# Scaling the norm's rows on ScalarE, and the norm's weights per partition behind the transposes

## The chip, the cores and the metric

The kernel runs on one core of a Trainium2 chip. A core has TensorE (PE: matrix products, written to PSUM), VectorE (DVE), ScalarE (ACT), GpSimd (POOL) and SyncE (SP, which here issues all the transfers). Each engine runs its own instructions strictly in the order in which they were issued and waits for the others by semaphores. The metric is the device time of one execution in microseconds; lower is better.

## What is computed

Three stages follow each other: a gated linear attention over 768 steps (2 batches, 8 heads of 40), a gated feed-forward layer behind an RMS norm, and a second feed-forward layer.

```python
y[:, :, t] = o * h_tilde / denom                        # attention, one step
x = attn_out.transpose(0, 2, 1, 3).reshape(1536, 320)   # tokens x (heads*40)
rms = np.sqrt(np.mean(x * x, axis=-1, keepdims=True) + 1e-06)
xn = x / rms * rms_g                                    # the norm, rms_g: 320 weights
g = xn @ w_gate                                         # 320 -> 1536
x = (g / (1 + np.exp(-g))) * (xn @ w_val) @ w_out       # 1536 -> 320
h = x @ w_in                                            # 320 -> 2048
out = np.maximum(0.01 * h, h) @ w_out2                  # 2048 -> 320
```

## The kernel before

The 1536 tokens are 12 tiles of 128 (`T` = 0 to 11, six chunks for each of the two batches). The attention is computed chunk by chunk; its result for a tile is `y`, with the tokens on the partitions and the 320 features along the row. The norm turns `y` into `xn`, PE transposes `xn` in three blocks of 128 columns into the PSUM tile `tp` (so that features lie on the partitions), and the result goes to `X`, split into a coarse part (`X[:, 0:3]`, the rounding to PE's fp32r format, done by ACT) and the rest (`X[:, 3:6]`, the difference, done by DVE). The third block holds the last 64 features twice: columns 320 to 383 of `xn` are a copy of columns 256 to 319.

The feed-forward layer takes the tiles in four groups of three (0-2, 3-5, 6-8, 9-11). An up-projection (line 646) is eight matmuls over the 384 tokens of a group, with three blocks of features in coarse and fine parts; the second matmul already reads the fine part of block 0, so a group can start only when all its three tiles have passed the norm.

All instructions are issued in one order written out by hand: `ORDER`, a list of some 1900 short tokens, played from the first to the last. A token is one helper with its indices, and the order on each engine is the order of its tokens. For one tile `T` the tokens of the norm are: `yr` (DVE: `y` divided by the denominator), `sq` (ACT: sum of squares), `y2.T.0` (DVE), `y2.T.1` (POOL: the power -0.5), `y2.T.2` (three small DVE instructions, which end in `z`, one scale per token), `xn` (line 488), `xc` (line 492), `tp` (line 499, PE), `xh` (line 503, ACT), `xl` (line 507, DVE). Between them stand the tokens of other tiles and stages; those the prediction comes to are:

- `p`, `av`, `inn`, `kv`: the attention's scores (DVE line 382), its products (PE lines 395, 405, 417); `eq` and `mask`: POOL's scaling of `eb` (line 359) and its masking of `Ab` (line 355); `st`, `cb`, `c`: the state C (DVE lines 426 and 428), its copy by ACT (lines 433 and 434), its decay on POOL (line 364); `arg`: ACT's exponentials (line 351);
- `U`, `T`, `E`, `M`, `S`, `L` with group and block of the hidden layer: up-projections (PE), tanh (ACT line 673), two products (DVE lines 678, 685), coarse and fine parts of the result (ACT line 694, DVE line 700); `D`: the down-projection (PE line 718);
- `a`, `r`, `b`: the unpacking of weights (ACT line 538 and DVE lines 536 and 540, then a coarse and a fine part); `id`: matmuls on a constant that nobody reads (line 226).

PSUM has buffers in pairs by tag. A `tp` tile takes a buffer of the tag "o" (for tiles 1 and 2 of the tag "gv"), which the attention's results of a tile (`o1`) use too, in turn. The norm's weights lie in `gb`, 128 x 320, the same row on every partition, fetched by one transfer (`dgb`, line 995).

Of the kernel before, what the change touches and what calls it, by code (L numbers as in the profile page):

```python
# [56 lines left out]
co.1.1.2 cv.1.1.2 cv.0.2.6 sq.0 y2.0.0 yr.1 wA.2 kv.1 dgb p.2.0 av.2.0 arg.2.1 y2.0.1 p.2.1 y2.0.2 k.2 sq.1 y2.1.0 a.2  # L57
y2.1.1 a.1 xn.0 a.2 arg.3.1 a.1 dq.3 qk.3 p.3.1 dq.4 cb.0 wB.1 a.2 xc.0 b.1 dsl y2.1.2 th.2 a.2 dr.2.6 da.4 mask.4.1
wA.4 xn.1 av.2.1 inn.2 y1.2 xc.1 id.1 st.1 abs.2 id.1 id.1 id.1 p.3.0 rec.2 tp.0 id.1 b.1 tp.1 dn.3 yr.2 dr.1.2
mask.4.0 dc.1.2 a.4 sq.2 b.1 y2.2.0 kv.2 xh.1 wR.3 th.3 de.3 dE.2.6 k.3 b.1 id.1 xh.0 xl.0 av.3.0 co.1.2.6 cv.1.2.6  # L60
xl.1 cb.1 y2.2.1 y2.2.2 r.3 qk.4 eq.3 av.3.1 inn.3 dv.1.2 xn.2 arg.4.0 xc.2 tp.2 abs.3 r.3 r.3 c.3 rec.3 dn.5 kv.3 a.4
xh.2 arg.4.1 xl.2 U.0.1.1 p.4.0 k.5 y1.3 da.5 a.4 st.3 U.0.1.0 cb.3 p.4.1 th.5 T.0.1 dn.4 th.4 mask.5.0 wA.3 yr.3 sq.3
a.4 E.0.1 mask.5.1 a.3 arg.5.1 dc.2.6 de.4 r.3 arg.5.0 y2.3.0 a.3 eq.4 M.0.1 av.4.0 av.4.1 inn.4 dq.5 qk.5 y2.3.1 y1.4
p.5.1 U.0.0.0 p.5.0 T.0.0 E.0.0 dv.2.6 U.0.0.1 M.0.0 da.6 mask.6.1 arg.6.1 de.5 wB.0 abs.4 dq.6 a.3 rec.4 mask.6.0
av.5.0 av.5.1 S.0.1 eq.5 y2.3.2 yr.4 S.0.0 inn.5 kv.5 abs.5 b.0 xn.3 rec.5 b.0 sq.4 y2.4.0 y2.4.1 arg.6.0 qk.6 L.0.1
p.6.1 U.0.2.0 p.6.0 U.0.2.1 T.0.2 E.0.2 c.2 y1.5 dq.7 b.0 c.5 st.5 qk.7 yr.5 y2.4.2 c.4 cb.5 sq.5 a.3 k.4 kv.4 id.1
xc.3 tp.3 xh.3 y2.5.0 y2.5.1 dq.8 xn.4 da.7 xc.4 M.0.2 wB.2 U.0.3.0 st.4 cb.4 y2.5.2 c.6 L.0.0 xn.5 xl.3 tp.4 xh.4
xl.4 U.0.3.1 S.0.2 xc.5 T.0.3 tp.5 xh.5 de.6 dn.6 av.6.0 E.0.3 xl.5 av.6.1 wB.3 M.0.3 L.0.2 eq.6 inn.6 abs.6 wA.5 b.0
b.3 U.1.0.0 T.1.0 E.1.0 U.1.0.1 M.1.0 U.1.1.0 da.8 U.1.2.0 b.3 mask.7.0 arg.7.0 p.7.0 dn.7 av.7.0 mask.7.1 arg.7.1
p.7.1 av.7.1 k.7 S.0.3 b.2 L.0.3 de.7 b.2 eq.7 S.1.0 b.2 inn.7 L.1.0 b.2 b.3 b.3 wB.4 rec.6 T.1.2 E.1.2 mask.8.1 a.5  # L70
da.9 mask.9.0 mask.9.1 b.4 qk.8 a.5 th.7 T.1.1 th.6 y1.6 D.0.0.2 E.1.1 D.0.0.1 K.0.0.1 U.1.2.1 M.1.2 U.1.1.1 arg.8.1
p.8.1 M.1.1 mask.8.0 D.0.0.0 S.1.1 L.1.1 yr.6 S.1.2 a.5 wA.7 U.1.3.0 a.5 L.1.2 arg.8.0 b.4 p.8.0 de.9 dq.9 kv.7 T.1.3
E.1.3 k.6 eq.9 kv.6 st.6 arg.9.1 cb.6 U.1.3.1 M.1.3 abs.7 a.7 dn.8 a.7 U.0.5.0 T.0.5 E.0.5 sq.6 qk.9 K.0.0.0 av.8.0
de.8 S.1.3 L.1.3 wB.7 k.8 av.8.1 a.7 a.7 wR.5 K.0.0.2 rec.7 b.4 b.4 eq.8 inn.8 wA.6 a.6 a.6 dn.9 c.7 wB.6 de.11 y2.6.0
y2.6.1 b.6 U.0.4.0 U.0.5.1 M.0.5 y1.7 yr.7 D.1.0.0 y2.6.2 arg.9.0 p.9.0 D.1.0.1 T.0.4 U.0.4.1 S.0.5 L.0.5 E.0.4
# [1020 lines left out]
```

## Time and profile before

| | |
|---|---|
| three timed executions | 445.22, 447.4 and 451.2 us; median 447.4 us |
| profiled execution | 449.2 us from the first to the last instruction, 9736 instructions |
| PE busy | 437.8 us (97%) |
| DVE busy | 365.8 us (81%) |
| ACT busy | 281.3 us (63%) |
| POOL busy | 102.1 us (23%) |

The profile shows one execution, and times in it run from its first instruction. What lies around that span is not shown for it; of the timed runs two are shorter than the span and one is longer. The norm's instructions lie between 31.7 us and 163.8 us; what follows is the two feed-forward layers. PE's busy share is high because its matmuls are pipelined and nearly always queued. The granted clock of PE is given as a share of 2.4 GHz.

### The profile page before, as it was taken

What the parts mean: (1) busy time and instruction counts of PE and PEld (TensorE: products, weight loads), DVE (VectorE), ACT (ScalarE), POOL (GpSimd) and SP (SyncE); (2) the same over time, 40 slices, a digit from 0 to 9 for tenths busy, and PEclk for the clock granted to TensorE, in tenths of its full rate; (3) what the DMA queues carried; (4) which work ended last, traced back from release to release, by engine and by line L of the source; (5) the groups of instructions that cost most, each with busy time, mean ns of one, the idle gap of its engine ahead of it and who ended that gap; (6) DMA issues with size and microseconds to landing.
All of it is one profiled execution on the core that took longest, in us unless ns stands there. A gap on an engine that the chain in (4) does not pass through costs nothing.

```text
span 449.2 us, 9736 instructions
## 1 busy us (share of the span) xinstructions
PE 437.8 (97%) x3720; PEld 415.7 (93%) x3720; DVE 365.8 (81%) x822; ACT 281.3 (63%) x709; POOL 102.1 (23%) x162
## 2 busy tenths in 40 slices
...
GB/s 267 316 265 283 251 287 119 265 232 82 248 88 77 56 0 175 78 83 0 124 1 1 1 1 0 1 1 153 30 31 76 107 47 32 31 29 31 0 2 176
DMA packets 21039, 45.47 MB, mean 101 GB/s; under 512 B 2128, under 2 KB 9168, under 8 KB 20992
## 3 DMA queue, kind: packets, MB, share of 16 engines
...
q8 instruction: 29, 0.48, 0.5%
q14 instruction: 18, 0.15, 0.1%
HBM read 42.79 MB, written 2.06 MB: 100 GB/s over the span
## 4 chain that ended last, share of the span: by engine, by line
PE 89%; DVE 6%; ACT 2%; issue 2%; DVEq 0%; ACTq 0%
PE h L796 13%; PE xa L718 10%; PE g L646 8%; PE v L646 8%; PE oa L969 6%; PE oa L968 6%; PE oa L967 6%; PE u L796 6%; PE xw L736 5%; PE s L335 3%; PE h L802 2%; PE h L801 2%; PE o L395 2%; PE busy L226 2%; PE o L405 1%
## 5 line engine op out<-in xcount | busy, mean ns | idle before, releaser
L969 PE MATMUL oa<-wB,xl 128*128 128x320 f32 x192 | 59.3, 309 | 0.0
L968 PE MATMUL oa<-wB,xh 128*128 128x320 f32 x192 | 59.3, 309 | 0.0
L967 PE MATMUL oa<-wB,xh 128*128 128x320 f32 x192 | 59.2, 308 | 0.0
L646 PE MATMUL g<-X,wA 128*128 128x384 f32 x256 | 50.7, 343 | 0.9 <-ACT th L671 0.4
L979 DVE TENSOR_TENSOR x<-oa,x 128x320 f32<-128x320 f32 x84 | 39.5, 484 | 14.6 <-PE oa L969 13.9
L646 PE MATMUL v<-X,wA 128*128 128x384 f32 x256 | 50.0, 339 | 0.1
L646 PEld LDWEIGHTS g<-X,wA 128*128 128x128 f32 x256 | 44.5, 189 | 2.9 <-ACT th L671 0.7
L718 PE MATMUL xa<-sh,wB 128*128 128x384 f32 x160 | 46.0, 338 | 0.0
L646 PEld LDWEIGHTS v<-X,wA 128*128 128x128 f32 x256 | 44.6, 188 | 0.7 <-DVE X L507 0.4
L578 POOL TENSOR_TENSOR sums<-w_A 128x128 f32<-128x128 f32 x8 | 3.9, 488 | 151.8 <-DVE w_A L540 146.6
L969 PEld LDWEIGHTS oa<-wB,xl 128*128 128x128 f32 x192 | 36.0, 188 | 0.1
L967 PEld LDWEIGHTS oa<-wB,xh 128*128 128x128 f32 x192 | 36.0, 188 | 0.0
L968 PEld LDWEIGHTS oa<-wB,xh 128*128 128x128 f32 x192 | 36.0, 188 | 0.0
L796 PE MATMUL h<-X,wA 128*128 128x384 f32 x144 | 32.2, 337 | 0.0
L718 PE MATMUL xa<-sl,wB 128*128 128x384 f32 x96 | 32.2, 336 | 0.0
L943 ACT ACTIVATE c<-c 128x384 f32<-128x384 f32 x48 | 25.2, 525 | 7.2 <-DVE c L840 3.4
L718 PEld LDWEIGHTS xa<-sh,wB 128*128 128x128 f32 x160 | 29.4, 188 | 0.1
L953 DVE TENSOR_TENSOR xl<-c,xh 128x384 fp32r<-128x384 f32 x48 | 26.1, 556 | 1.0 <-ACT xh L948 0.8
L948 ACT CAST xh<-c 128x384 fp32r<-128x384 f32 x48 | 24.3, 513 | 2.9 <-PE oa L968 2.2
L351 ACT ACTIVATE w<-Ab,aeu 128x128 f32<-128x128 f32 x80 | 25.3, 392 | 0.6 <-POOL Ab L355 0.6
L796 PEld LDWEIGHTS h<-X,wA 128*128 128x128 f32 x144 | 25.0, 188 | 0.1
L479 POOL TENSOR_TENSOR sm<-sm,mhalf 128x1 f32<-128x1 f32 x12 | 8.0, 663 | 65.0 <-DVE sm L477 65.0
...
## 6 DMA issues: line engine op xcount, KB each, us to landing
...
```

Source lines behind the costliest of these rows:

```text
L351: A.activation(w[:, j], src, AF.Exp, scale=-1.0, bias=col)
L646: PE.matmul(dst, a, x, start=(i == 0), stop=(i == len(seq) - 1))
L718: PE.matmul(xa, w, x, start=(k == 0), stop=(k == len(seq) - 1))
L736: PE.matmul(xas["w", g, i], a, x, start=(f == NE and k == 0), stop=(f == NF - 1 and k == len(seq) - 1),)
L796: PE.matmul(dst, x, y, start=first and j == 0, stop=j == 2, skip_group_check=not first)
L943: A.activation(t, src, AF.Prelu, alpha=0.01)
L948: A.copy(v["h"], v["t"])
L953: V.tensor_tensor(v["l"], v["t"], v["h"].bitcast(F32), op=ALU.subtract)
L967: PE.matmul(oa, v["h"][:, ts], wb[:, 0:DM], start=m == 0, stop=False)
L968: PE.matmul(oa, v["h"][:, ts], wb[:, DM:], start=False, stop=False)
L969: PE.matmul(oa, v["l"][:, ts], wb[:, 0:DM], start=False, stop=m == 1)
L979: V.tensor_tensor(dst, oas[k, p, i], dst, op=ALU.add)
```

## The change

Instead of DVE, ACT multiplies the rows of `y` by `z`, in two instructions (320 columns and the 64 that stand twice), each with one scale per partition. The weights come behind the transposes, where a feature is a partition: `gcol`, 128 x 3, one column per block. ACT's `xh` takes them as a scale in three instructions of 128 columns in place of one of 384, and DVE's `xl` multiplies by them and subtracts, also in three. The token `xc` is gone and `dgb` is `dgc`; the order of all other tokens is the same, and the two ACT instructions of the new `xn` stand where the old `xn` stood in the list.

```diff
-    gb = attc.tile([128, DM], F32, name="gb")
+    gcol = attc.tile([128, 3], F32, name="gcol")
...
     def att_xna(T):
...
-        V.scalar_tensor_tensor(out=xn[:, 0:DM], in0=t["yf"], scalar=t["z"], in1=gb, op0=ALU.mult, op1=ALU.mult)
-
-    def att_xnc(T):
-        xn = st_[T]["xn"]
-        A.copy(xn[:, DM:384], xn[:, 256:DM])
+        A.activation(xn[:, 0:DM], t["yf"], AF.Copy, scale=t["z"])
+        A.activation(xn[:, DM:], t["yf"][:, 256:], AF.Copy, scale=t["z"])
...
     def att_xh(T):
-        A.copy(X[:, 0:3, T * L:(T + 1) * L], st_[T]["tv"])
+        for k in range(3):
+            A.activation(X[:, k, T * L:(T + 1) * L], st_[T]["tv"][:, k], AF.Copy, scale=gcol[:, k:k + 1])
...
     def att_xl(T):
         tv, cs = st_[T]["tv"], slice(T * L, (T + 1) * L)
-        V.tensor_tensor(X[:, 3:6, cs], tv, X[:, 0:3, cs].bitcast(F32), op=ALU.subtract)
+        for k in range(3):
+            V.scalar_tensor_tensor(
+                out=X[:, 3 + k, cs], in0=tv[:, k], scalar=gcol[:, k:k + 1], in1=X[:, k, cs].bitcast(F32), op0=ALU.mult, op1=ALU.subtract,
+            )
...
-        dsl=lambda: Q.dma_start(out=sel, in_=cst2), dgb=lambda: Q.dma_start(out=gb, in_=rg.partition_broadcast(128)),
+        dsl=lambda: Q.dma_start(out=sel, in_=cst2), dgc=lambda: Q.dma_start(out=gcol, in_=rg),
...
-        "rg": c(moe_rms_g.reshape(DM)),
+        "rg": c(moe_rms_g[np.concatenate([s, s + 128, s % 64 + 256]).reshape(3, 128).T]),
```

In `ORDER` each of the twelve `xc` tokens is deleted, as here for tile 5:

```diff
-xl.4 U.0.3.1 S.0.2 xc.5 T.0.3 tp.5 xh.5
+xl.4 U.0.3.1 S.0.2 T.0.3 tp.5 xh.5
```

What stands in a row on ACT at tiles 3, 4 and 5, before (L470 is `sq.5`, L492 `xc`, L503 `xh`, L433 and L434 `cb.4`, L694 `S.0.2`, L673 `T.0.3`; xn_1043, xn_1144 and xn_1170 belong to tiles 3, 4 and 5):

```order
86 L470 ACTIVATE junk_1119,sm_1038<-y_1093 128x320
87 L492 COPY xn_1043<-xn_1043 128x64
88 L503 CAST X<-tp_1135 128x3x128
89 L492 COPY xn_1144<-xn_1144 128x64
90 L433 COPY Cbd_97<-C_95 64x4x41
91 L434 COPY Cbd_97<-C_95 40x4x41
92 L503 CAST X<-tp_1173 128x3x128
93 L694 CAST sh_2_1188<-th_2_1089 128x384
94 L492 COPY xn_1170<-xn_1170 128x64
95 L673 ACTIVATE th_3_1191<-g_3_1152 128x384
96 L503 CAST X<-tp_1193 128x3x128
```

And after (L488 and L489 are the new `xn`, L501 the new `xh`, L695 and L674 the old L694 and L673; xn_1158 belongs to tile 4 and xn_1184 to tile 5):

```order
91 L470 ACTIVATE junk_1132,sm_1050<-y_1106 128x320
92 L501 ACTIVATE X<-tp_1147,gcol 128x128 x3
93 L488 ACTIVATE xn_1158<-y_932,sm_974 128x320
94 L489 ACTIVATE xn_1158<-y_932,sm_974 128x64
95 L433 COPY Cbd_97<-C_95 64x4x41
96 L434 COPY Cbd_97<-C_95 40x4x41
97 L488 ACTIVATE xn_1184<-y_1106,sm_1050 128x320
98 L489 ACTIVATE xn_1184<-y_1106,sm_1050 128x64
99 L501 ACTIVATE X<-tp_1190,gcol 128x128 x3
100 L695 CAST sh_2_1209<-th_2_1102 128x384
101 L674 ACTIVATE th_3_1211<-g_3_1166 128x384
102 L501 ACTIVATE X<-tp_1213,gcol 128x128 x3
```

The copies of 64 columns are gone. The scaling of tile 4 stands between the `xh` of tile 3 and `cb.4`, that of tile 5 between `cb.4` and the `xh` of tile 4; tile 3's stands further up, behind line 539 of `b.0`.

What stands in a row on DVE at the same place, before (L481 to L483 are `y2.5.2`, L700 is `L.0.0`, L488 the old `xn` of tile 5, L507 the `xl` of tiles 3, 4 and 5, L678 `E.0.3`):

```order
142 L481 TENSOR_SCALAR sm_1038<-sm_1038 128x1
143 L482 TENSOR_SCALAR sm_1038<-sm_1038 128x1
144 L483 TENSOR_TENSOR sm_1038<-sm_1038 128x1
145 L700 TENSOR_TENSOR sl_0_1168<-th_0_933,sh_0_1012 128x384
146 L488 SCALAR_TENSOR_TENSOR xn_1170<-y_1093,sm_1038,gb 128x320
147 L507 TENSOR_TENSOR X<-tp_1135,X 128x3x128
148 L507 TENSOR_TENSOR X<-tp_1173,X 128x3x128
149 L678 SCALAR_TENSOR_TENSOR th_3_1191<-th_3_1191,g_3_1152 128x384
150 L507 TENSOR_TENSOR X<-tp_1193,X 128x3x128
```

And after (L506 is the new `xl`):

```order
137 L481 TENSOR_SCALAR sm_1050<-sm_1050 128x1
138 L482 TENSOR_SCALAR sm_1050<-sm_1050 128x1
139 L483 TENSOR_TENSOR sm_1050<-sm_1050 128x1
140 L701 TENSOR_TENSOR sl_0_1182<-th_0_945,sh_0_1024 128x384
141 L506 SCALAR_TENSOR_TENSOR X<-tp_1147,gcol,X 128x128 x3
142 L506 SCALAR_TENSOR_TENSOR X<-tp_1190,gcol,X 128x128 x3
143 L679 SCALAR_TENSOR_TENSOR th_3_1211<-th_3_1211,g_3_1166 128x384
144 L506 SCALAR_TENSOR_TENSOR X<-tp_1213,gcol,X 128x128 x3
```

Nothing stands between `L.0.0` and the `xl` of tile 3 any more.

## Rows read from the trace of the kernel before

**Rows 1.** Busy us (instructions) in three stretches: PE, PEld, DVE, ACT, POOL; clock, DMA, GB/s.

```profile
30.00:50.00 20.00, 17.89 (x289) 13.90 (x290) 16.77 (x49) 13.90 (x43) 8.99 (x16) 0.66 0.89 241
50.00:76.00 26.00, 23.51 (x445) 21.09 (x444) 25.19 (x56) 16.46 (x52) 14.24 (x20) 0.93 0.77 249
76.00:160.00 84.00, 84.00 (x1012) 80.86 (x1012) 63.93 (x162) 49.83 (x145) 16.79 (x27) 1.00 0.47 140
```

**Rows 2.** DVE's groups by line and shape: count, busy us, mean ns, idle before.

```profile
L488 DVE SCALAR_TENSOR_TENSOR xn<-y,sm,gb 128x320 f32<-128x320 f32 x12 | 9.2, 763 | 0.1
...
L507 DVE TENSOR_TENSOR X<-tp,X 128x384 fp32r<-128x384 f32 x12 | 6.5, 551 | 1.8 <-ACT X L503 1.8
...
L593 DVE TENSOR_TENSOR wA<-sums,wA 128x128 fp32r<-128x128 f32 x8 | 2.2, 281 | 0.0
```

**Rows 3.** ACT's groups by line and shape, 0 to 165 us.

```profile
L351 ACT ACTIVATE w<-Ab,aeu 128x128 f32<-128x128 f32 x80 | 25.3, 392 | 0.6 <-POOL Ab L355 0.6
...
L503 ACT CAST X<-tp 128x384 fp32r<-128x384 f32 x12 | 5.7, 477 | 4.0 <-PE tp L499 3.9
...
L439 ACT ACTIVATE nat<-nat 128x320 f32<-128x320 f32 x12 | 5.5, 465 | 0.1
...
L351 ACT ACTIVATE w<-A,aeu 128x128 f32<-128x128 f32 x16 | 4.5, 362 | 3.0 <-DVE x L231 1.6 <-PE pt L248 1.0 <-PE A L261 0.4
...
L492 ACT COPY xn<-xn 128x64 f32<-128x64 f32 x12 | 2.9, 241 | 6.2 <-DVE xn L488 6.2
```

**Rows 4.** The chain that ended last, 64 to 76 us: start, us, what.

```profile
67.42 2.63 issue
...
73.72 1.93 PE g L646 x8
```

**Rows 5.** All engines in order of time, 64 to 74 us, with idle time before.

```profile
65.13 0.48 ACT L503 CAST X<-tp 128x384 fp32r<-128x384 f32 x1 [0.53 <-PE tp L499]
...
66.04 0.33 ACT L433 COPY Cbd<-C 64x164 f32<-64x164 f32 x1 [0.28 <-DVE C L426]
...
66.59 1.65 PE L646 MATMUL v<-X,wA 128*128 128x384 f32 x8
...
66.95 3.17 DVE L488 SCALAR_TENSOR_TENSOR xn<-y,sm,gb 128x320 f32<-128x320 f32 x1
67.32 1.28 POOL L359 TENSOR_TENSOR eb<-eb,qkt 128x512 f32<-128x512 f32 x1
...
68.56 1.22 POOL L355 TENSOR_SCALAR_AFFINE_SELECT Ab<-Ab 128x512 f32<-128x512 f32 x2
...
70.73 0.64 PE L499 MATMUL tp<-consts,xn 128*128 128x128 f32 x3 [2.49 <-DVE X L507]
```

**Rows 6.** The same view, 40 to 52 us.

```profile
40.94 1.28 POOL L359 TENSOR_TENSOR eb<-eb,qkt 128x512 f32<-128x512 f32 x1 [0.46 <-DMA eb<-e_d]
...
41.25 0.56 DVE L507 TENSOR_TENSOR X<-tp,X 128x384 fp32r<-128x384 f32 x1 [0.70 <-ACT X L503]
...
49.70 1.29 POOL L359 TENSOR_TENSOR eb<-eb,qkt 128x512 f32<-128x512 f32 x1
49.76 1.58 DVE L464 TENSOR_TENSOR y<-y,sm 128x320 f32<-128x320 f32 x1
```

**Rows 7.** Windows again: PE's clock behind two pauses.

```profile
41.00:47.00 6.00, 6.00 (x126) 5.08 (x125) 3.79 (x13) 3.53 (x13) 1.85 (x2) 0.50 0.94 267
71.00:74.00 3.00, 3.00 (x100) 2.48 (x99) 2.59 (x6) 0.69 (x3) 1.19 (x3) 0.50 0.17 42
```

**Rows 8.** PE in order of time, 36 to 42 us.

```profile
37.13 0.55 PE L499 MATMUL tp<-consts,xn 128*128 128x128 f32 x3 [0.41 <-DVE C L428]
...
39.45 0.35 PE L295 MATMUL pg<-rG,sel 16*128 16x8 f32 x2 [1.22 <-issue]
```

**Rows 9.** The chain that ended last, 160 to 170 us.

```profile
162.83 0.38 ACT X L503
...
168.08 1.28 ACT L671
```

More of the change, by code (lines that the diff above doesn't have):

```diff
@@ L56 @@
 rec.0 wA.1 a.1 rec.1 r.2 dq.2 a.1 yr.0 id.1 mask.3.0 arg.3.0 r.2 id.1 r.2 qk.2 th.1 st.0 y1.1 de.2 dA.2.6 eq.2 ux.1.2
[L57 to L75, printed above, removed]
@@ new lines @@
+y2.1.1 a.1 xn.0 a.2 arg.3.1 a.1 dq.3 qk.3 p.3.1 dq.4 cb.0 wB.1 a.2 b.1 dsl y2.1.2 th.2 a.2 dr.2.6 da.4 mask.4.1 wA.4
+xn.1 av.2.1 inn.2 y1.2 id.1 st.1 abs.2 id.1 id.1 id.1 p.3.0 rec.2 tp.0 id.1 b.1 tp.1 dn.3 yr.2 dr.1.2 mask.4.0 dc.1.2
+a.4 sq.2 b.1 y2.2.0 kv.2 xh.1 wR.3 th.3 de.3 dE.2.6 k.3 b.1 id.1 xh.0 xl.0 av.3.0 co.1.2.6 cv.1.2.6 xl.1 cb.1 y2.2.1
+y2.2.2 r.3 qk.4 eq.3 av.3.1 inn.3 dv.1.2 xn.2 arg.4.0 tp.2 abs.3 r.3 r.3 c.3 rec.3 dn.5 kv.3 a.4 xh.2 arg.4.1 xl.2
+U.0.1.1 p.4.0 k.5 y1.3 da.5 a.4 st.3 U.0.1.0 cb.3 p.4.1 th.5 T.0.1 dn.4 th.4 mask.5.0 wA.3 yr.3 sq.3 a.4 E.0.1
@@ new lines @@
+mask.5.1 a.3 arg.5.1 dc.2.6 de.4 r.3 arg.5.0 y2.3.0 a.3 eq.4 M.0.1 av.4.0 av.4.1 inn.4 dq.5 qk.5 y2.3.1 y1.4 p.5.1
+U.0.0.0 p.5.0 T.0.0 E.0.0 dv.2.6 U.0.0.1 M.0.0 da.6 mask.6.1 arg.6.1 de.5 wB.0 abs.4 dq.6 a.3 rec.4 mask.6.0 av.5.0
+av.5.1 S.0.1 eq.5 y2.3.2 yr.4 S.0.0 inn.5 kv.5 abs.5 b.0 xn.3 rec.5 b.0 sq.4 y2.4.0 y2.4.1 arg.6.0 qk.6 L.0.1 p.6.1
+U.0.2.0 p.6.0 U.0.2.1 T.0.2 E.0.2 c.2 y1.5 dq.7 b.0 c.5 st.5 qk.7 yr.5 y2.4.2 c.4 cb.5 sq.5 a.3 k.4 kv.4 id.1 tp.3
+xh.3 y2.5.0 y2.5.1 dq.8 xn.4 da.7 M.0.2 wB.2 U.0.3.0 st.4 cb.4 y2.5.2 c.6 L.0.0 xn.5 xl.3 tp.4 xh.4 xl.4 U.0.3.1 S.0.2
@@ new lines @@
+T.0.3 tp.5 xh.5 de.6 dn.6 av.6.0 E.0.3 xl.5 av.6.1 wB.3 M.0.3 L.0.2 eq.6 inn.6 abs.6 wA.5 b.0 b.3 U.1.0.0 T.1.0 E.1.0
+U.1.0.1 M.1.0 U.1.1.0 da.8 U.1.2.0 b.3 mask.7.0 arg.7.0 p.7.0 dn.7 av.7.0 mask.7.1 arg.7.1 p.7.1 av.7.1 k.7 S.0.3 b.2
+L.0.3 de.7 b.2 eq.7 S.1.0 b.2 inn.7 L.1.0 b.2 b.3 b.3 wB.4 rec.6 T.1.2 E.1.2 mask.8.1 a.5 da.9 mask.9.0 mask.9.1 b.4
+qk.8 a.5 th.7 T.1.1 th.6 y1.6 D.0.0.2 E.1.1 D.0.0.1 K.0.0.1 U.1.2.1 M.1.2 U.1.1.1 arg.8.1 p.8.1 M.1.1 mask.8.0 D.0.0.0
+S.1.1 L.1.1 yr.6 S.1.2 a.5 wA.7 U.1.3.0 a.5 L.1.2 arg.8.0 b.4 p.8.0 de.9 dq.9 kv.7 T.1.3 E.1.3 k.6 eq.9 kv.6 st.6
```

186 lines of the change are left out of this document (95 added, 91 removed).

## The prediction

> **What bounds the kernel now.** I read the busy shares by stretch first, then the chain of work that ended last, then the timeline around each of the twelve tiles. The norm's instructions all lie before 164 us, and the stretches there differ [rows 1]. From 76 to 160 us PE is busy for 84.00 of 84 us at a granted clock of 1.00 (its 2.4 GHz level): nothing that DVE or ACT saves there is seen, as long as neither comes late. From 50 to 76 us DVE is busy for 25.19 of 26 us, ACT for 16.46, and PE misses 2.5 us. From 30 to 50 us PE misses 2.1 us and runs at 0.66 of the clock on average. So only 30 to 76 us, and the end of the stage at 160 to 170 us, can give or take time.
>
> Inside them one place stands out. From 67.42 us the chain goes through 2.63 us in which nothing that the profile shows was awaited [rows 4]. The timeline says what that is: DVE's `xn` of tile 5 stood there, from 66.95 us, and took 3.17 us [rows 5], where the twelve take 9.2 us together, so that the other eleven take (9.2 - 3.17) / 11 = 0.55 us each [rows 2]. While it stood, POOL ran `eq` and `mask` (67.32 to 69.78 us) without a gap. PE had finished its up-projection at 66.59 + 1.65 = 68.24 us and waited 2.49 us for the PSUM buffer of `tp.5`, which the `xl` of tile 3 gives back, and that `xl` stood behind this `xn` on DVE [rows 5]. After the pause PE was granted 0.50 (1.2 GHz) from 71 to 74 us, with work in all three of those us [rows 7]; at the other level this work takes half, so the pause cost another 1.5 us. This place alone is worth up to 2.49 + 1.5 = 4.0 us.
>
> Which DVE instructions POOL holds up is seen in two pairs [rows 6]. The `yr` at 49.76 us, beside POOL's line 359, took 1.58 us; it reads two tiles from SBUF. The `xl` at 41.25 us, inside the same POOL instruction of another tile, took 0.56 us, its usual time [rows 2]; it reads one tile from PSUM and one from SBUF. The old `xn` is of the first kind (`y` and `gb`).
> The Trainium skill (SBUF — State Buffer, Who interferes with whom) has a rule for this: a DVE instruction with two SBUF inputs contends with a GpSimd instruction that reads SBUF and waits for all of it, one with a single SBUF input does not. By it the stall leaves with the old `xn` and the sum below holds; without it the next DVE instruction could inherit the stall, and the first rival below would be the forecast. Both pairs agree with it.
>
> **The change part by part.**
>
> DVE, `xn` and `xl`. Removed: twelve `xn`, 0.55 us each, one of them 3.17 [rows 2, 5]. Added: each `xl` is three instructions of 128 columns in place of one of 0.551 us. No row shows this form; the nearest of that width took 0.281 us [rows 2], so three take between 0.55 us (no cost for the splitting) and 0.84 us. I take the upper end, +0.29 us. DVE gains about 0.26 us a tile, and the 2.6 us of the stall.
>
> ACT, `xn`. The 320 columns without a scale per partition took 0.465 us, 64 columns 0.241 us [rows 3]; on the line between them 128 columns would take 0.297 us, and line 351, which has one operand per partition (its bias), took 0.392 us. So such an operand costs 0.095 us here. New `xn`: 0.465 + 0.095 + 0.241 + 0.095 = 0.90 us, some 0.85 us with the overlap of neighbours; bounds 0.71 and 0.90. The old copy (0.24 us) goes.
>
> ACT, `xh`. Three of 128 columns out of PSUM: line 351 with PSUM input took 0.362 us alone and 4.5 / 16 = 0.28 us in a row [rows 3], so 0.36 + 2 x 0.28 = 0.92 us in place of 0.48; bounds 0.8 and 1.1. Together ACT gets some 1.0 to 1.3 us more per tile, 12 to 15 us in all, where it now has 16.46 us in 26 [rows 1]. ACT has room on average; the question is its order.
>
> The transfer. 160 KB of `gb` become 1.5 KB while the transfers are busy for 0.89 of their time [rows 1]. At 241 GB/s that is 0.7 us less traffic; no wait of PE in this stretch ends with a transfer, so I count nothing, between -0.7 and 0.
>
> **Place B, tiles 3 to 5 (60 to 76 us).** The old times are carried forward with the new durations. `xh.3` starts at 65.13 us, when PE has made `tp.3` [rows 5], and ends at 66.05. ACT then scales tile 4 until 66.9; `tp.4`, which before came just ahead of the up-projection at 66.59 us [rows 5], and that up-projection with it, come 0.5 us later. ACT copies the state (`cb.4`, two of 0.33 us [rows 5]), scales tile 5 until 68.4 us, and starts `xh.4`. DVE, without the old `xn`, starts `xl.3` at 67.0 us and is done at 67.8. PE's up-projection now ends at 68.24 + 0.5 = 68.75 us, and both things that `tp.5` needs, its rows (68.4) and its buffer (67.8), are there: the 2.49 us are gone. The next wait is that of `av.6` for the buffer of `tp.4`, which `xl.4` gives back: `xh.4` ends at 69.3 and `xl.4` at 69.6 us, `tp.5` at 69.1, so 0.5 us. Of POOL's work `inn.6` needs `eq.6`; that waits for `cb.4` and moves from 68.6 to 69.3 us, ahead of its use. Without a pause of two us the clock should hold. Sum: -2.49 - 1.5 + 0.5 + 0.5 = -3.0 us; the group's up-projection, at 73.72 us before [rows 4], starts some 2.7 us earlier and also runs at the higher clock. Bounds: -4.0 (no new waits) and 0 (the new waits are as long as the old one, and the clock falls with them).
>
> **Place A, tiles 0 to 2 (30 to 50 us).** PE waited 0.41 us at `tp.0` for DVE's copy of the state and 1.22 us ahead of line 295, which reads a product of DVE [rows 8]. Both DVE instructions stand behind the old `xn` of tiles 0 and 1, so they come up to 0.5 us earlier each time. But `arg.3.1` on ACT now stands behind the new `xn.0`, and `p.3.1` on DVE waits for it: the first saving is lost, the second stays. I take -0.4 us, the length of the first pause; bounds -1.6 (both pauses go) and +0.5 (`arg.4.0` stands behind `xn.2`, which waits for `z` of tile 2).
>
> **Place C, the end of the stage (160 to 170 us).** Here ACT is on the chain: `xh.11` at 162.83 us, then the unpacking of weights between ACT and DVE, up to the load of ACT's function table at 168.08 us [rows 9]. `xh.11` is 0.45 us longer and everything behind it moves: +0.5 us; bounds 0 (PE can start the group on the first block) and +0.8 (`xl.11` longer, too).
>
> From 76 to 160 us I count nothing: PE is never idle there [rows 1], and the slack of the six tiles' `xn` and `xh` is the time that ACT is free, 34 of 84 us, against some 8 us more work.
>
> Sum: -3.0 - 0.4 + 0.5 = -2.9 us on a span of 449.2 us. Median before 447.4 us, so **444.5 us**; bounds by the ends -5.6 and +1.3: 441.8 and 448.7 us. The profiled span lies 1.8 us above the median of the three timed executions, which themselves reach from 445.22 to 451.2; a difference of 2% (9 us) is about what this kernel's measurement tells from no change.
>
> **The rivals.**
>
> The next wait takes the gain. If the stall is not the two inputs' but POOL's hold on whatever DVE issues next, `xl.3` inherits it, or `tp.5` or `av.6` waits for something that the trace hides behind the old wait. For: DVE is busy for 25.19 of 26 us, so its relief of 0.26 us a tile buys little. Against: the undisturbed `xl` [rows 6]. Place B gives 0, A and C cancel: 447.4 us, 447 to 448.
>
> ACT becomes late, and the kernel slower. Place B again: `xn.5` now stands on ACT behind `xh.3`, `xn.4` and `cb.4`, and `tp.5` waits for ACT instead of DVE. It decides from the point at which ACT ends `xn.5` after 70.1 us, when the old one ended; I have 68.4, so ACT would have to be 1.7 us later than I think, for instance because it waits in order for a `z` that DVE or POOL brings late. Then the pause and the fall of the clock stay, the extra 0.5 us at `tp.4` and 0.5 us at C come on top, and another +0.5 us at `arg.4.0`, with at most 1.5 us for a second fall of the clock: +1.5 to +3, 449 to 450.5 us, taken as 449.7. Against it: ACT was idle for 10 of 26 us.
>
> The clock rises early. Place A's pauses are followed by a stretch at the lower level, 0.50 from 41 to 47 us with PE busy for all six [rows 7]. If the pauses shrink enough for the higher level to stay, some 3 us more go: 441.5 us. Against: most of the longer pause is left by my count.
>
> That the change does not do what it says is no case of its own: `xn` and `xl` are on their engines in any schedule, since the list sets it, and `gcol` is fetched where `gb` was, while its first use (`xh.1`) comes later than that of `gb` did.
>
> **How the numbers follow.** Forecast 0.55, the gain is taken 0.18, ACT late 0.15, clock 0.12. The time is the likeliest's, 444.5 us. The range, with the scatter of the timed executions (-0.5% and +0.8%) over the cases' bounds, is 439.5 to 450 us: it leaves out the upper end of the slow case and what lies beyond the clock case. Faster by over 2% needs 438.5 us or less, which only the clock case with everything else at its good end comes near: 0.05. Slower by over 2% needs 456.3 us, past every case: 0.03. Within 2%: 0.92.
>
> **What would show it.** No DVE instruction over 1 us between 66 and 70 us of the old count; PE's pause at `tp.5` under 0.5 us; the clock at 1.00 through the next stretch; DVE's busy time down by some 5 us and ACT's up by 10 to 15; a pause of some 0.5 us at `tp.4` whose releaser is ACT; the table load some 2.5 us earlier than 168.08. The prediction is wrong if the pause at `tp.5` is still two us long, if ACT's new `xn` waits for `z` at many tiles, or if PE pauses between 76 and 160 us.

## The result and the profile after

The changed kernel takes 450.76 us (median of 20 executions, 448.67 to 455.79), the kernel before 449.03 us beside it (20 executions, 444.73 to 451.88). The ratio is 1.0053, with a 95% interval from 1.0028 to 1.0079: some 1.3 to 3.5 us slower. The forecast was 444.5 us. The profiled execution has a span of 450.2 us and took 452.01 us. The ratio, here and in the table of the experiments, takes only executions within 1.5% of the fastest of their kernel, which in the table leaves out a third or more of the kernel before's, so the medians of all executions stand beside it there, and where the two disagree I go by the medians.

The busy times moved as counted: DVE from 365.8 to 359.7 us, ACT from 281.3 to 291.6. Part 1 of the page of the changed kernel:

```profile
PE 434.5 (97%) x3718; PEld 414.0 (92%) x3720; DVE 359.7 (80%) x834; ACT 291.6 (65%) x745; POOL 101.9 (23%) x162
```

So did the prices. The groups of the four new steps (count, busy us, mean ns, idle before): three pieces of `xh` take 0.86 to 0.89 us where 0.92 was taken, three of `xl` 0.87 (0.84), `xn` 0.56 + 0.34 = 0.90 (0.90). That the price was right says nothing yet about what stands behind each piece.

```profile
L501 ACT ACTIVATE X<-tp,gcol 128x128 fp32r<-128x128 f32 x36 | 10.5, 365 | 3.5 <-PE tp L496 3.5
...
L488 ACT ACTIVATE xn<-y,sm 128x320 f32<-128x320 f32 x12 | 6.7, 561 | 2.8 <-DVE sm L483 2.6
...
L489 ACT ACTIVATE xn<-y,sm 128x64 f32<-128x64 f32 x12 | 4.0, 336 | 0.0
...
L506 DVE SCALAR_TENSOR_TENSOR X<-tp,gcol,X 128x128 fp32r<-128x128 f32 x36 | 10.4, 344 | 6.7 <-ACT X L501 6.7
```

The windows (columns as in [rows 1]) show where PE now stands. DVE has 6.0 us less to do from 50 to 76 us, and PE still misses 3.6 us of 26 there, more than before; from 30 to 50 us it misses 4.6. The two last rows give the clock behind the two places: it was low for a part of 45 to 50 us and of 70 to 75 (0.69 and 0.70; in the kernel before 0.79 and 0.66). Time missed is not yet time lost, since the clock from 30 to 50 us was 0.80 and not 0.66. What was lost is seen between fixed points of the program: from `av.1` (the long row of line 395, at 18.29 us here and 20.67 before) to `tp.3` it is 45.85 us against 43.94, from there to the next up-projection 8.86 against 9.04, on to the first matmul of line 719 (line 718 before) 9.42 against 8.65, and on to the table load of place C 86.97 against 85.78: 3.7 us in all. This execution reached `av.1` 2.4 us sooner, and other kernels with the same start do not (20.64 to 20.69 us in three), so the two spans, 450.2 and 449.2 us, show less of the loss than there is.

```profile
30.00:50.00 20.00, 15.42 (x266) 12.07 (x266) 14.60 (x45) 14.90 (x47) 8.25 (x12) 0.80 0.85 253
50.00:76.00 26.00, 22.41 (x436) 20.11 (x432) 19.16 (x57) 17.74 (x59) 12.54 (x19) 0.93 0.69 224
76.00:160.00 84.00, 83.78 (x1009) 80.13 (x1008) 61.64 (x161) 54.06 (x157) 16.49 (x26) 1.00 0.45 140
...
45.00:50.00 5.00, 4.70 (x32) 4.20 (x34) 3.70 (x9) 3.23 (x10) 2.61 (x4) 0.69 0.45 159
...
70.00:75.00 5.00, 3.27 (x55) 2.85 (x42) 2.75 (x8) 0.56 (x2) 2.83 (x4) 0.70 0.06 15
```

Place B in order of time. `tp.5` comes at 67.88 us without a pause (70.73 after 2.49 in [rows 5]); `av.6` (line 395) waits 0.98 us for `xl.4`. Then something new: PE does 19 of the 32 matmuls of `inn.6` (line 405), stops for 1.73 us with nothing awaited that the profile shows, and goes on. The group's up-projection starts at 73.00 us, against 73.65 in the same view of the kernel before (the chain of [rows 4] has 73.72).

```profile
67.88 0.49 PE L496 MATMUL tp<-consts,xn 128*128 128x128 f32 x3
...
68.42 0.87 DVE L506 SCALAR_TENSOR_TENSOR X<-tp,gcol,X 128x128 fp32r<-128x128 f32 x3 [1.36 <-ACT X L501]
...
69.34 0.81 PE L395 MATMUL o<-nat,w 128*32 128x41 f32 x64 [0.98 <-DVE X L506]
...
69.99 0.59 PE L405 MATMUL o<-Cbd,eb 104*32 104x82 f32 x19
...
72.30 0.77 PE L405 MATMUL o<-Cbd,eb 104*32 104x82 f32 x13 [1.73 <-issue]
...
73.00 1.33 PE L647 MATMUL g<-X,wA 128*128 128x384 f32 x3
```

Place A, the same view, has a chain of waits that the kernel before does not have. ACT stands 1.42 us at `xn.2`, waiting for `z` of tile 2; PE waits 1.44 us for that `xn`; `arg.4.0` (line 351, 1.26 us) could have run in ACT's wait but is queued behind it, and so PE waits 0.90 us more for the ACT instruction behind `arg.4.0`; then 0.44 for `xh.2` and 0.30 for `xl.2`. By then the clock is low, and seven matmuls of the first up-projection take 2.61 us. (The kernel before had a low clock near here too, from 41 to 47 us [rows 7], but its first up-projection, at 47.48 us, came behind that: 2.09 us for all eight.)

```profile
41.42 0.56 ACT L488 ACTIVATE xn<-y,sm 128x320 f32<-128x320 f32 x1 [1.42 <-DVE sm L483]
...
42.04 0.57 PE L496 MATMUL tp<-consts,xn 128*128 128x128 f32 x3 [1.44 <-ACT xn L488]
42.13 1.26 ACT L351 ACTIVATE w<-Ab,aeu 128x128 f32<-128x128 f32 x4
...
43.50 0.66 PE L417 MATMUL o<-nat,Kt 128*64 128x41 f32 x16 [0.90 <-ACT sm L444]
...
44.60 0.60 PE L647 MATMUL v<-X,wA 128*128 128x384 f32 x1 [0.44 <-ACT X L501]
...
45.51 2.61 PE L647 MATMUL v<-X,wA 128*128 128x384 f32 x7 [0.30 <-DVE X L506]
```

Place C. ACT's table load is at 169.39 us, 1.31 later than in [rows 9], and PE waits 0.79 us behind it (0.41 before). From the first matmul of line 719 (82.42 us) to that load it is 86.97 us; in the kernel before 82.30 to 168.08, 85.78: +1.2 us. The chain shows two `xh` in it, of tiles 10 and 11, each in three pieces.

```profile
161.97 0.77 ACT X L501 x3
...
163.54 0.79 ACT X L501 x3
```

### The profile page after: what moved, and what is told of

It reads as the page before. It is cut to its first block, busy times and chain, and to the rows that moved or that the text cites. A ratio compares the mean times of both kernels' runs of the same rounds, so it can differ in the third digit from the quotient of the medians.

```text
span 450.2 us, 9782 instructions
## 1 busy us (share of the span) xinstructions
PE 434.5 (97%) x3718; PEld 414.0 (92%) x3720; DVE 359.7 (80%) x834; ACT 291.6 (65%) x745; POOL 101.9 (23%) x162
## 4 chain that ended last, share of the span: by engine, by line
PE 85%; DVE 7%; ACT 5%; issue 2%; DVEq 0%; ACTq 0%
PE h L797 13%; PE xa L719 9%; PE v L647 8%; PE g L647 8%; PE oa L970 6%; PE oa L969 6%; PE oa L968 6%; PE u L797 6%; PE xw L737 5%; PE s L335 2%; PE h L803 2%; PE h L802 2%; PE o L395 2%; PE busy L226 2%; ACT X L501 1%
## 5 line engine op out<-in xcount | busy, mean ns | idle before, releaser
L647 PE MATMUL v<-X,wA 128*128 128x384 f32 x256 | 51.4, 346 | 1.0 <-ACT X L501 0.4
L647 PEld LDWEIGHTS g<-X,wA 128*128 128x128 f32 x256 | 45.5, 193 | 3.5 <-ACT th L672 1.1
```

Source lines behind the costliest of these rows:

```text
L647: PE.matmul(dst, a, x, start=(i == 0), stop=(i == len(seq) - 1))
```

## The experiments

Fourteen kernels, each beside the kernel before on the same chip, twelve executions each (nine of xn_on_act_whole_pieces and new_tile_5), 23 to 35 of the kernel before. The executions of one kernel scatter: those of the kernel before run from 441.87 to 453.65 us. Drawing the executions anew at random gives most of the differences of medians an uncertainty of one to two us, and more to those of xn_on_act_whole_pieces and new_tile_5_moved_blocks.

| run | median us | kernel before beside it | difference | ratio, 95% interval |
|---|---|---|---|---|
| after_moved_blocks | 450.22 | 448.88 | +1.3 | 1.0081, 1.0041 to 1.0121 |
| before_moved_blocks | 448.93 | 448.88 | 0.0 | 0.9994, 0.9962 to 1.0026 |
| rows_on_dve | 448.69 | 448.88 | -0.2 | 0.9981, 0.9954 to 1.0008 |
| xn_on_act_whole_pieces | 445.73 | 448.88 | -3.2 | 0.9923, 0.9882 to 0.9964 |
| new_tiles_0_to_2 | 452.55 | 449.66 | +2.9 | 1.0064, 1.0040 to 1.0088 |
| new_tiles_3_to_5 | 446.81 | 449.66 | -2.9 | 0.9940, 0.9909 to 0.9972 |
| new_tile_5 | 446.06 | 449.66 | -3.6 | 0.9950, 0.9903 to 0.9996 |
| new_tile_5_moved_blocks | 446.88 | 449.66 | -2.8 | 0.9923, 0.9887 to 0.9958 |
| tiles_0_to_2_xn2_later | 450.33 | 449.48 | +0.9 | 1.0024, 0.9993 to 1.0054 |
| tiles_0_to_2_idle_matmuls | 449.94 | 449.48 | +0.5 | 1.0026, 0.9997 to 1.0054 |
| tiles_0_to_2_rows_only | 448.41 | 449.48 | -1.1 | 0.9984, 0.9948 to 1.0020 |
| tile_5_idle_matmuls | 446.47 | 449.48 | -3.0 | 0.9976, 0.9934 to 1.0019 |
| new_tiles_6_to_11 | 449.70 | 449.11 | +0.6 | 1.0064, 1.0030 to 1.0098 |
| change_with_place_a_mended | 447.57 | 449.11 | -1.5 | 1.0035, 1.0001 to 1.0068 |

**First group: is it the stop in `inn.6`, or the pieces?** The trace suggested that PE waited for its own instructions there. The queue that the page marks "instruction" moved 29 packets in the whole run (packets, MB, share of 16 engines; the page's part 3), 0.48 MB for PE's 7438 instructions, and one of them began in the tenth of a us at 69.20 us, among data packets, and kept one of the 16 engines for 0.883 x 16 x 0.1 = 1.4 us (second row, the transfers' view of 69.20 to 69.30 us of the changed kernel).

```profile
q8 instruction: 29, 0.48, 0.4%
...
q8 instruction: 1, 0.02, 88.3%
```

after_moved_blocks and before_moved_blocks, the control:

```diff
-id.1 id.1 id.1 id.1 did cr id.1 id.1 dfg dig id.1 id.1 id.1 wR.1
+ts.64 did cr id.1 dfg dig id.1 id.1 wR.1
+    def tiny(n):
+        dst = psum("busy", "acc")
+        for _ in range(n):
+            PE.matmul(dst[0:32, 0:32], idle[0][:, 0:32], idle[1][:, 0:32], start=True, stop=True)
```

> The changed kernel, with 6 of the first idle matmuls of 512 columns replaced by 64 of 32 columns: 116 more PE instructions at the very start, none later, all else the same. Theory F (fetch): PE's 1.73 us stop in the middle of inn.6 waits for PE's own next instructions. The queue marked instruction moved 29 packets of 16 KB in a run of 7,438 PE instructions, so about 256 a packet; one packet began at 69.20 us, behind data transfers that kept the engines busy, and the stop began at 70.58. With 116 instructions more ahead of it the limit between two packets falls 116 instructions earlier in the program, inside av.6, and the packet is called for some 6 us earlier: no stop over 0.4 us in inn.6, the clock at 1.00 from 70 to 75 us, 1.7 to 2.5 us less than the changed kernel, ratio to the kernel before 0.997 to 1.001. Rival D (data): the stop belongs to that matmul of inn.6, for instance to POOL's eb or the state; then it stays at the 20th matmul with 1.2 us or more, and the ratio stays at 1.003 to 1.008. Rival L (the place only moves): a stop as long appears in av.6, ratio as under D.

> The kernel before with the same 116 PE instructions more at the start: the control for the run above. Theory F: the 2.49 us at tp.5 cover whatever packet is due there, so nothing is to be won: ratio 0.998 to 1.003 and the pause at tp.5 stays at 2 to 2.6 us. If the start itself costs or gives time, this run shows how much, and the run above has to be read against it. Rival D says the same of this kernel.

The stop went away, as theory F expected: in the timeline of after_moved_blocks (its lines are five further down) `inn.6` runs through and the up-projection follows at once.

```profile
71.51 0.78 PE L410 MATMUL o<-Cbd,eb 104*32 104x82 f32 x32
72.22 1.66 PE L652 MATMUL g<-X,wA 128*128 128x384 f32 x8
```

From `tp.3` to that up-projection it is 6.55 us, against 8.86 in the changed kernel and 9.04 before: that is the 2.5 us that place B was to give. But the time did not fall below the kernel before: +1.3 us, where F had 0.997 to 1.001. So F was right on the stop and wrong on the whole. In the control the pause at `tp.5` stays (2.47 us) and the time is that of the kernel before, as expected. (In both kernels with moved blocks a few executions took 451 to 453 us at a mean clock of 0.98 to 0.99; no trace shows one of them, and what the moved start does there is open.)

rows_on_dve:

```diff
-        A.activation(xn[:, 0:DM], t["yf"], AF.Copy, scale=t["z"])
-        A.activation(xn[:, DM:], t["yf"][:, 256:], AF.Copy, scale=t["z"])
+        V.tensor_scalar(out=xn[:, 0:DM], in0=t["yf"], scalar1=t["z"], scalar2=None, op0=ALU.mult)
```

> The changed kernel's weights behind the transposes (three pieces each of xh and xl), but the rows are scaled by DVE in an instruction with one SBUF tile as input (y by the column z), and ACT copies the last 64 columns as before; the order is that of the kernel before. Theory F with my reading of POOL: the new xn takes 0.32 to 0.40 us at every tile, tile 5 too, so the 2.49 us pause goes as in the changed kernel; ACT is free of 0.65 us a tile, so the 1.44 us wait of tp.2 for ACT is under 0.6 us; the end of the stage still pays 0.9 us for the pieces, and a stop in inn.6 for instructions may come back, since nothing moves the packets. Ratio 0.996 to 1.003. Rival: if POOL holds any DVE instruction, xn of tile 5 takes over 2 us again and the pause stays: 1.002 to 1.006.

The group of `xn` shows 380 ns on average, and its longest took 388 ns. The pause at `tp.5` is gone. PE stops in `inn.6` again, one matmul later and for 0.49 us (fourth row; the rows behind the first are its timeline). In time the kernel equals the kernel before.

```profile
L488 DVE TENSOR_SCALAR xn<-y,sm 128x320 f32<-128x320 f32 x12 | 4.6, 380 | 0.2
...
68.88 0.38 DVE L488 TENSOR_SCALAR xn<-y,sm 128x320 f32<-128x320 f32 x1
...
69.70 1.29 POOL L359 TENSOR_TENSOR eb<-eb,qkt 128x512 f32<-128x512 f32 x1
...
72.94 0.48 PE L405 MATMUL o<-Cbd,eb 104*32 104x82 f32 x12 [0.49 <-issue]
```

That POOL leaves a DVE instruction with one SBUF tile as input alone is not shown by this, as no `xn` of this run met POOL's `eq` or `mask`: that of tile 5 ended 0.4 us before `eq` began (second and third row). Elsewhere such an instruction was held: the unpacking of line 536 reads one tile from SBUF and took 1.41 us in the kernel before, beside a POOL instruction, where it takes 0.32 alone. What the prediction says of one input is too wide for this kernel. What POOL left alone in every trace is the `xl`, which reads one tile from PSUM and one from SBUF: 0.54 to 0.56 us whole and 0.34 to 0.35 us a piece, with POOL at work or not.

```profile
205.78 1.49 POOL L872 TENSOR_TENSOR both<-wA 128x512 f32<-128x512 f32 x1
206.04 1.41 DVE L536 TENSOR_SCALAR w_B<-raw_B 128x320 uint32<-128x320 uint32 x1
```

The expectation missed place A: `tp.2` was to wait under 0.6 us and waits 1.57, now for DVE's `xn`, which stands behind `xl.0` and `xl.1`. The clock falls there too, and the same seven matmuls take 2.61 us. From `av.1` to `tp.3` it is 46.40 us (43.94 before), and from there to the up-projection 6.27 (9.04): place A loses what place B gives, with no `xn` on ACT. So in this trace the pieces are enough for it.

```profile
44.70 0.66 PE L499 MATMUL tp<-consts,xn 128*128 128x128 f32 x3 [1.57 <-DVE xn L488]
...
47.45 2.61 PE L650 MATMUL v<-X,wA 128*128 128x384 f32 x7 [0.22 <-DVE X L509]
```

xn_on_act_whole_pieces:

```diff
-        for k in range(3):
-            A.activation(X[:, k, T * L:(T + 1) * L], st_[T]["tv"][:, k], AF.Copy, scale=gcol[:, k:k + 1])
+        A.copy(X[:, 0:3, T * L:(T + 1) * L], st_[T]["tv"])
```
(and `xl` one `tensor_tensor` of 384 columns, as before; the norm's weights are left out)

> The changed kernel with xh and xl whole again, one instruction of 384 columns each; the norm's weights are left out altogether. It has the rows' scaling on ACT alone. Theory F: the stall of the old xn is gone, the end of the stage (148 to 180 us) loses its 0.9 us, xh takes 0.48 us and xl 0.55 us, but PE still stops for instructions in or near inn.6, 1 us or more: ratio 0.998 to 1.003. Rival P (the pieces cost it all): the ratio falls to 0.993 to 0.996, 3 us under the kernel before, as was forecast for place B, and no stop over 0.5 us appears in inn.6.

Both theories were half right. The median is what rival P expected, 3.2 us under the kernel before; it is the least certain of all, since three of the nine executions took 449.87 to 452.33 us. Yet the profiled execution has the stop in `inn.6` at the same matmul, 1.59 us long, as F expected. The stop exists, and nothing here shows it in the median.

```profile
72.36 0.48 PE L405 MATMUL o<-Cbd,eb 104*32 104x82 f32 x13 [1.59 <-issue]
```

**Second group: which tiles?** One edit of the kernel before, with the set of tiles that take the new form (`xh`, `xl` and the copy alike); both `gb` and `gcol` are fetched:

```diff
+NEW = (0, 1, 2)
+        if T in NEW:
+            A.activation(xn[:, 0:DM], t["yf"], AF.Copy, scale=t["z"])
...
+        else:
             V.scalar_tensor_tensor(out=xn[:, 0:DM], in0=t["yf"], scalar=t["z"], in1=gb, op0=ALU.mult, op1=ALU.mult)
```

> The change in tiles 0 to 2 alone; tiles 3 to 11 in the form of the kernel before, so both forms of the weights are loaded. Theory A (place A costs what place B gives): from the first long row of line 395 to tp.3 the kernel before took 43.9 us, the changed kernel 45.9, so this one takes 45 to 46.5 us there, with waits of tp.2 for ACT's xn and of the matmuls behind it for ACT (0.9 us at line 417), and the clock falls to 0.50 just when the first up-projections run. The pause of 2.5 us at tp.5 stays. About 2 us over the kernel before: ratio 1.002 to 1.008. Rival B (all the loss is PE's stop in inn.6): ratio 0.997 to 1.002, and 43 to 44.5 us up to tp.3.

> The change in tiles 3 to 5 alone, the other nine in the form of the kernel before. Theory A: place B comes out as in the changed kernel, from tp.3 to the group's up-projection 6.5 us where PE need not wait for instructions, up to 8.9 us where it must, against 9.0 to 9.3 before; place A and the end of the stage as before. Ratio 0.993 to 0.999. Rival B: the stop in inn.6 takes all of it, ratio 0.998 to 1.002. Rival P (the pieces cost more than the rows): 0.999 to 1.004.

This separates the places: +2.9 us for tiles 0 to 2, -2.9 for tiles 3 to 5. In new_tiles_0_to_2 the waits of place A are there again, with the clock at 0.50 behind them (its timeline, and then windows of 2 us):

```profile
41.00 0.86 DVE L522 SCALAR_TENSOR_TENSOR X<-tp,gcol,X 128x128 fp32r<-128x128 f32 x3
...
42.26 0.16 DVE L485 TENSOR_TENSOR sm<-sm 128x1 f32<-128x1 f32 x1
...
43.12 0.57 PE L506 MATMUL tp<-consts,xn 128*128 128x128 f32 x3 [0.89 <-ACT xn L491]
...
44.59 0.66 PE L419 MATMUL o<-nat,Kt 128*64 128x41 f32 x16 [0.90 <-ACT sm L446]
...
46.59 2.61 PE L663 MATMUL v<-X,wA 128*128 128x384 f32 x7 [0.22 <-DVE X L522]
```

```profile
47.00:49.00 2.00, 2.00 (x7) 2.00 (x7) 2.00 (x6) 1.42 (x5) 1.68 (x2) 0.50 0.32 123
49.00:51.00 2.00, 2.00 (x8) 2.00 (x8) 0.88 (x2) 0.52 (x2) 0.00 (x0) 0.50 0.94 271
```

Its twelve times lie close together, 451.43 to 453.7 us, at the upper end of those of the kernel before beside it (443.66 to 452.05). The single profile hides this: from `av.1`, the long row of line 395 at 18 to 21 us, to `tp.3` it shows 44.87 us for this run, and with an unchanged place A 41.69 (new_tile_5_moved_blocks) to 45.91 (new_tiles_6_to_11) in six traces. With an unchanged place A the clock there differs from execution to execution (0.79, 0.66 and 1.00 from 45 to 50 us in the traces of before, of before_moved_blocks and of new_tile_5_moved_blocks); with the new tiles 0 to 2 the short times are gone. That the scatter goes with the clock is seen in the mean granted clock of each execution: of 122 executions of the kernel before, the 32 with the lowest (under 0.959) took 448.6 to 453.65 us, the 24 with the highest (0.971 and more) 441.87 to 448.78. Those of new_tiles_0_to_2 had 0.955 to 0.966.

In new_tiles_3_to_5 place B is as drawn up in the prediction, and here PE has no stop; from `tp.3` to the up-projection it is 6.56 us:

```profile
69.36 0.81 PE L397 MATMUL o<-nat,w 128*32 128x41 f32 x64 [1.00 <-DVE X L522]
70.01 0.78 PE L407 MATMUL o<-Cbd,eb 104*32 104x82 f32 x32
70.72 1.49 PE L663 MATMUL g<-X,wA 128*128 128x384 f32 x7
```

> The change in tile 5 alone, whose old xn stood 3.17 us on DVE. xh and xl of tiles 3 and 4 are whole, so tp.4 and av.6 no longer wait for pieces. Theory A: tp.5 waits under 0.4 us and av.6 under 0.3 us, PE reaches inn.6 sooner than in any run so far, so the stop for instructions is the longest yet or about 1.7 us; from tp.3 to the group's up-projection 6.0 us without a stop, 7.5 to 8.5 us with one. Ratio 0.992 to 0.999. Rival H (POOL holds whatever DVE issues next): xl.3 takes over 2 us and the pause stays, ratio 0.998 to 1.002.

> The change in tile 5 alone and the 116 more PE instructions at the start. Theory A with theory F: no stop in inn.6, from tp.3 to the group's up-projection 6.0 to 6.6 us, 2.5 to 3.5 us under the kernel before: ratio 0.991 to 0.996, the best of all. If the stop is not worth anything in the whole, this run and the one without the moved blocks agree within 0.002.

The one tile whose `xn` stood on DVE is enough: -3.6 us, the best median, and better than both kernels. Rival H fails: `xl.3` behind the removed `xn` took 0.55 us with POOL at work. With moved blocks the stop (0.64 us in new_tile_5, where the longest yet was expected) is gone, and the time is the same within its scatter: the stop is worth nothing that these medians show. "The best of all" was wrong.

**Third group: what in place A costs?** All in tiles 0 to 2 alone, but the last. tiles_0_to_2_xn2_later moves one token; the two kernels with idle matmuls leave that order and add `id.3` behind `inn.3`, `id.4` behind `tp.2` and `id.2` behind `xl.2`; tiles_0_to_2_rows_only has the whole `xh` and `xl` and leaves the weights out in its three tiles.

```diff
-dv.1.2 xn.2 arg.4.0 xc.2 tp.2
+dv.1.2 arg.4.0 xn.2 xc.2 tp.2
```

> The change in tiles 0 to 2 alone, with one step moved: xn of tile 2 stands on ACT behind arg.4.0 (its four exponentials, 1.26 us) and not ahead of it. In the run of tiles 0 to 2 ACT stood 1.44 us at this xn, waiting for z, with arg.4.0 and abs.3 behind it, and PE then waited 0.90 us for abs.3. Theory A: ACT works through the wait, tp.2 comes at the same time, the 0.90 us at line 417 fall under 0.2 us and the up-projection starts 1 us sooner; ratio 1.001 to 1.005 where the unmoved one had 1.0064. Rival K (the clock alone decides, and any pause lets it fall): no gain, 1.005 to 1.009.

> The change in tiles 0 to 2 alone, with nine idle matmuls (3, 4 and 2) put into the three waits of PE ahead of the first up-projections (before tp.2, before line 417, before the up-projection). Theory K (the waits cost 2.2 us, but the fall of the clock to 0.50 through 47 to 52 us costs the other 2 us): the clock stays at 1.00 from 45 to 52 us, the two up-projections take 1.6 us each and not 3, ratio 0.997 to 1.003, in place of 1.0064. Rival A alone (only the waits count): ratio 1.004 to 1.009, since the idle matmuls can only add.

> Rows scaled by ACT in tiles 0 to 2, with xh and xl whole in all tiles; the norm's weights are left out of tiles 0 to 2. It tells the pieces from the rows in place A. Theory A: the pieces (0.87 us of DVE for xl.0 and xl.1 ahead of z of tile 2, and xh.0 to xh.2 0.4 us longer) bring some half of it: ratio 1.000 to 1.005, tp.2 some 0.6 us sooner than with pieces, the 0.90 us at line 417 still there. Rival P (pieces alone): 0.996 to 1.001.

> The change in tile 5 alone with the same nine idle matmuls in place A, whose work is that of the kernel before. Theory K: in executions in which the clock fell at 45 to 50 us it now holds, so the slower half of the times goes: ratio 0.986 to 0.993, median 443 to 445.5 us. Rival: PE has no wait there in most executions and the idle matmuls push the up-projection back by up to 1.9 us: 0.995 to 1.000.

tiles_0_to_2_xn2_later: theory A holds. ACT works through the wait, and PE's 0.90 us at line 419 are gone; +0.9 us in place of +2.9. `tp.2` does not come at the same time, though: it waits 1.65 us, for an `xn` that could start only at 43.05 us, behind `z`. In this trace the clock falls as before, and the seven matmuls take 2.61 us. Two rows of its timeline:

```profile
41.51 1.26 ACT L353 ACTIVATE w<-Ab,aeu 128x128 f32<-128x128 f32 x4
43.05 0.56 ACT L491 ACTIVATE xn<-y,sm 128x320 f32<-128x320 f32 x1 [0.28 <-DVE sm L485]
```

tiles_0_to_2_idle_matmuls: theory K holds. `tp.2` still waits 0.89 us and the up-projection 0.46 us for `xl.2`, but the clock stays at 1.00, and the same seven matmuls take 1.48 us in place of 2.61: +0.5 us in place of +2.9. Its timeline and a window:

```profile
47.30 1.48 PE L663 MATMUL v<-X,wA 128*128 128x384 f32 x7 [0.46 <-DVE X L522]
```

```profile
47.00:49.00 2.00, 1.70 (x10) 1.70 (x11) 2.00 (x7) 1.53 (x5) 2.00 (x3) 1.00 0.03 10
```

tiles_0_to_2_rows_only: the pieces are what tips place A. Without them it is -1.1 us, no loss that shows (rival P), though the 0.90 us for ACT are still there, as A had it. The reason stands in its timeline: each `xl` takes 0.55 us and not 0.87, and the last step of `z` starts at 41.46 us and not at 42.26. (In this trace, too, the clock falls behind the waits: eight matmuls of the first up-projection take 3.20 us.)

```profile
40.51 0.55 DVE L519 TENSOR_TENSOR X<-tp,X 128x384 fp32r<-128x384 f32 x1
41.46 0.16 DVE L485 TENSOR_TENSOR sm<-sm 128x1 f32<-128x1 f32 x1
```

tile_5_idle_matmuls: theory K promised 443 to 445.5 us and got 446.47, the time without the idle matmuls. The clock is 1.00 from 41 to 56 us in its trace, but over twelve executions they give nothing where place A is as before: there a held clock and the time of the idle matmuls themselves can cancel, as the rival had it, which is not shown.

**Fourth group: the rest of the sum.**

> The change in tiles 6 to 11 alone. Theory A: nothing up to 80 us; from the first block of line 719 at 82 us to the load of ACT's function table before the last groups, 85.8 us in the kernel before and 87.0 in the changed one, this one takes 86.7 to 87.1; the pause of 2.5 us at tp.5 stays. 0.5 to 1.2 us slower, ratio 1.000 to 1.004. Rival Z (what the six tiles put on ACT is hidden, and the late place is the earlier ones' echo): 85.6 to 86.0 us there, ratio 0.997 to 1.001.

> The changed kernel in all twelve tiles, with both remedies at place A: xn of tile 2 behind arg.4.0 on ACT, and nine idle matmuls in PE's three waits there. Theory A with theory K: the clock holds at 1.00 from 45 to 53 us, place A costs under 0.5 us, place B gives its 2 to 3 us (less by a stop for instructions of up to 1.7 us), the end of the stage costs 0.5 to 1.2 us: 1 to 3 us under the changed kernel's 1.0053, ratio 0.995 to 1.002. Rival: places do not add up, the time stays over 1.003.

new_tiles_6_to_11: +0.6 us by the medians; the ratio, 1.0064, lies above what either theory had. From the first matmul of line 719 in its numbering (735), at 84.26 us, to the table load, in the row below, it is 86.95 us: the late place is the late tiles' own, rival Z fails. For this stretch the traces are sharper than the times: 86.94 to 87.00 us in the four with the new form in tiles 6 to 11, 85.73 to 85.93 in the ten with the old one. The two halves of the change show in it as well: 86.23 with the rows on ACT and whole pieces, 86.46 with the rows on DVE and three pieces.

```profile
171.21 1.28 ACT L688 ACT_TABLE_LOAD   x1
```

change_with_place_a_mended is the whole change with the moved `xn.2` and the nine idle matmuls: 447.57 us, by the medians 1.5 under the kernel before, as theory A had it; the ratio, 1.0035, is the rival's, so whether it beats the kernel before stays open. Against the changed kernel it is clear: its twelve executions took 445.3 to 448.64 us, all twenty of the changed kernel 448.67 or more, though not side by side. In its trace it is 56.90 us from `av.1` to the first matmul of line 719, against 64.13 in that of the changed kernel, and the clock held:

```profile
45.00:50.00 5.00, 5.00 (x109) 4.51 (x112) 4.53 (x10) 4.27 (x13) 3.30 (x5) 1.00 0.50 169
```

## Why the prediction was wrong

Its sum was -3.0 (B) - 0.4 (A) + 0.5 (C). The runs of parts give -2.9, +2.9 and +0.6 by the medians, +0.6 together (+1.2 with place C as the traces have it), and the whole +1.7; with an uncertainty of one to two us on each that closes, no closer. Of the 6.3 us between 444.5 and 450.76, 4.6 are this sum's; 1.6 are the start of it, a median of three executions (447.4 us) where twenty gave 449.03.

- **The failed step is place A**: "I take -0.4 us ... bounds -1.6 (both pauses go) and +0.5 (`arg.4.0` stands behind `xn.2`, which waits for `z` of tile 2)". Measured is +2.9. The two pauses that it counted did shrink (in the changed kernel 0.41 us to none, with two new ones of 0.24 and 0.33 ahead of it, and 1.22 to 0.93); the loss comes behind them, at `xn.2`. Three things were missing. The pieces were priced in DVE's total ("DVE gains about 0.26 us a tile") and on place B's chain, never on place A's, where `xl.0` and `xl.1` stand right ahead of the three small instructions that make `z` of tile 2; with the longer `xh` they bring it 0.8 us later, and in the trace of rows_on_dve this alone is enough. `arg.4.0` was seen, but put at 0.5 where PE waited 0.90. And the price of a pause was taken as its length, though for place B the prediction itself had counted the clock behind a pause; here the pauses lie just ahead of the group's first up-projections, which then ran at 0.50. Any one of three remedies (the pieces whole, `xn.2` later, idle matmuls) takes away 2 us or more; their effects overlap, and how much of the 2.9 us is the waits and how much the clock is not settled, as the clock fell in the traces of the first two as well.
- **Place B was right in mechanism and size**: -3.0 forecast, -2.9 measured (tiles 3 to 5 alone). The stall of the old `xn` is no accident of one execution: in all seven traces that have it in tile 5 it took 3.16 to 3.17 us. The 2.49 us at `tp.5` went; the wait of `av.6` for `xl.4` was 0.98 us, not 0.5. At `tp.4` about 0.25 us were lost, not 0.5: the up-projection behind it starts 1.99 us after the one ahead, 1.74 before. The stop in `inn.6` was not foreseen as such; "`tp.5` or `av.6` waits for something that the trace hides behind the old wait" is its nearest description, and in the profiled execution it took the gain. The medians with and without it (new_tile_5 and its run with moved blocks) do not show it.
- **Place C was under-sized**: +0.5 forecast, +1.2 in the traces, +0.6 in the medians. Only `xh.11` was counted; the chain holds `xh.10` and `xl.11` in pieces, too (0.7 us with the rows on DVE), and the late tiles' `xn` now stands on ACT as well (0.45 us with whole pieces).
- **The rival "ACT becomes late"** came nearest in the number (449 to 450.5 against 450.76) and had the kind of wait, ACT in order behind a `z`, but put it at `xn.5`. It happened at `xn.2`. That its number was near is luck: it had the gain of place B gone, which was there.
- **The anchor hid the loss.** With the 1.8 us that lie around the span (452.01 - 450.2 in the changed kernel) the profiled execution of the kernel before took some 451 us, where all its executions run from 441.87 to 453.65. Its clock was at 0.50 from 41 to 47 us [rows 7], so no row of it could show what an execution that keeps its clock in place A has to lose. That the change takes those short executions away is read from the times and mean clocks; no trace shows one execution of the same kernel beside another.
- The signs named in the prediction came half true: no DVE instruction over 1 us between 64 and 72 us and no pause at `tp.5`, and the busy times as said, but the clock fell, and the table load came 1.31 us later and not 2.5 earlier.
